# Sliding-window attention and a spectral mix on one core: whole-batch loads, 128x192 band tiles, weights stationary in the mode mix, and x@w_ch moved under the weight stream

## The chip, the core and the metric

The kernel runs on one core of one Trainium2 chip. The metric is device time in microseconds (us) from start to end of the program, and lower is better. The span that the profile shows is 1 to 3 us shorter than that time.

Engine names: PE is TensorE (matmuls), PEld its weight loads, DVE is VectorE, ACT is ScalarE, POOL is GpSimd, SP is SyncE. A matmul has a stationary operand, loaded into the array of 128 x 128 cells, and a moving operand whose columns are streamed through it. "Array shape 128x64" below means a stationary operand of 128 rows and 64 columns.

## What is computed

```python
# q, k, v: (8 batches, 8 heads, 576 positions, 64), fp32
scores = q @ k.T / 8;  keep only 0 <= i - j < 64;  attn = softmax(scores) @ v
x  = attn laid out as (8, 576, 512)
X  = rfft(x over positions)[:, :64]                   # 64 modes
Yr = Xr @ w_r[m] - Xi @ w_i[m];  Yi = Xr @ w_i[m] + Xi @ w_r[m]     # per mode m
y  = irfft(Y);  u = x + y
out = u + relu(u @ w_ch)                              # fp32, (8, 576, 512)
```

The weights w_r and w_i are 2 x 64 matrices of 512 x 512 in fp32: 128 tiles of 1 MiB, turned into bf16 by the loads. They are most of the traffic. No mode can be mixed before the last batch's DFT, because each mode needs all 8 batches.

## The kernel before

Three stages run one after the other. Line numbers such as L228 in the profile lines of before are those of this kernel.

```python
# ---- attention, per batch b and pair of heads hp (cut) ----
for hh in range(2):                       # q and k: rows of one token, 256 B each
    nc.gpsimd.dma_start(out=raw[:, :, hh, :],
        in_=src5[b, 2*hp+hh, 0:512, :].rearrange("(c t) d -> t c d", t=128))
for c in range(4):                        # L192: 128x128 transposes
    nc.tensor.transpose(out=ptr[:, c*128:(c+1)*128], in_=raw2, identity=ident_bf)
...                                       # v: fp32 by SP, then a cast on ACT
for c in range(5):                        # key blocks of 128, 256 queries each
    nc.tensor.matmul(out=pss[:nk, :nq], lhsT=kT[pp, q0:q0+nk], rhs=qT[pp, q0:q0+nq])   # L228
    nc.scalar.activation(out=et, in_=pss, func=Exp, scale=1/8)                         # L235
    nc.vector.tensor_tensor(out=et, in0=et, in1=m01, op=mult)                          # L237
for qb in range(5):                       # weigh v: two matmuls add into pso
    nc.tensor.matmul(out=pso, lhsT=et_c[:nk, 0:nq2], rhs=vt[:nk, qb, :], start=True, ...)      # L247
    nc.tensor.matmul(out=pso, lhsT=et_p[:nk, 128:128+nq2], rhs=vt[:, qb-1, :], stop=True)      # L253
    ...                                   # reciprocal, scale: one pair of DVE instructions each
# DFT: trigF stationary, x moving (512 columns), L267, then 4 transposes

# ---- mode mix: X stationary (16 columns), weights moving (512 columns) ----
for m in range(64):                       # 20 buffers for weight tiles
    nc.gpsimd.dma_start(out=wr, in_=moe_w_r[m]...)
    nc.gpsimd.dma_start(out=wi, in_=moe_w_i[m]...)
    for dch in range(4):
        nc.tensor.matmul(out=psm, lhsT=XQ[:, dch, m, B:3*B], rhs=wr[:, dch, :])   # L323
        nc.tensor.matmul(out=psm, lhsT=XQ[:, dch, m, 0:2*B], rhs=wi[:, dch, :])   # L325
    ...                                   # copy to SBUF, two 8 KB DMAs into Yall

# ---- tail, per batch and 128 positions ----
#  inverse DFT (L344), u = x + y on DVE (L350), 4 transposes of u (L353), copy on ACT,
#  4 products with w_ch (L360), out = max(., 0) + u on DVE (L367), store
```

The softmax here doesn't subtract the row's maximum and nothing guards it: scores larger than these inputs give would overflow.

## Time and profile before

| | before |
|---|---|
| time, median of 3 | 644.14 us (643.96 to 644.51) |
| last DFT product ends | 277.9 us |
| mode mix, first to last matmul | 280.0 to 562.5 us |
| tail (to the end of the span) | 562.5 to 641.3 us |
| matmuls | 2160 |

First the slices of the page: the span is cut into 40 equal slices of 16 us, and each digit is the busy share in tenths. PEclk is the clock that the throttle granted to TensorE, DMA the mean busy share of the 16 DMA engines.

```profile
PE   1798859787888888889555565665565555579997
PEclk9999999999999999999767888657888778889999
DMA  9999999999893942019999999999999999614333
```

One sees three stages, and a hole in the DMA row just before the middle one: all 20 weight buffers are full, and the stream can't go on before the last DFT.

Next, three stretches of before. The columns are the stretch in us, its length, then for each engine its busy time and the number of instructions, the granted clock (1.00 is full speed), the DMA share and the GB/s moved.

```profile
core 0: us, PE busy (x) PEld busy (x) DVE busy (x) ACT busy (x) POOL busy (x), PEclk, DMA share, GB/s
90.00:120.00 30.00, 26.01 (x154) 13.26 (x154) 18.86 (x113) 21.78 (x67) 20.02 (x38) 1.00 1.10 124
300.00:400.00 100.00, 58.14 (x180) 17.74 (x178) 0.00 (x0) 12.83 (x23) 21.13 (x40) 0.81 1.07 215
600.00:620.00 20.00, 19.94 (x105) 13.53 (x105) 16.28 (x26) 5.28 (x9) 0.00 (x0) 1.00 0.37 136
```

Attention keeps PE, ACT and DVE all fairly busy; the middle is full on DMA (share above 1 because packets overlap); the tail is full on PE.

The chain of waits (the work that ended last, followed back from the end) in the middle. The columns are start, length, and what the chain waited on; "issue" is a stretch in which the engine waited for nothing that the profile shows.

```profile
243.42 40.75 issue
...
287.67 9.89 DMA wi<-in_moe_w_i_dram
298.09 19.70 DMA wi<-in_moe_w_i_dram
318.32 19.59 DMA wi<-in_moe_w_i_dram
```

The chain is 40 us of nothing (the hole), then loads alone, 20.2 us for each 8 tiles here and 20.1 on average.

Last, single PE instructions of before in order of time: start, duration, line, what it writes and reads, array shape, moving shape, count. What matters is the distance between two starts, because matmuls are pipelined and the durations overlap.

```profile
121.52 0.24 PE L247 MATMUL pso<-vt,et 128*128 128x65 bf16 x1 [0.27 <-DVE x_sb L259]
121.57 0.25 PE L253 MATMUL pso<-vt,et 128*128 128x65 bf16 x1
...
122.99 0.26 PE L247 MATMUL pso<-vt,et 64*64 64x65 bf16 x1
123.18 0.26 PE L253 MATMUL pso<-vt,et 128*64 128x65 bf16 x1
123.37 1.03 PE L267 MATMUL psX<-x_sb,trigF 128*128 128x512 bf16 x2
```

Two matmuls of the same array shape start 0.05 us apart (121.52, 121.57). When the shape changes, the next one starts 0.19 us later (122.99, 123.18, 123.37), with the same 65 columns to stream.

### The profile page before, as it was taken

Reading aid. Unit: us, or ns where it says so; the run is one execution under the profiler, and the core shown is the slowest. Engines: PE = TensorE matmul, PEld = TensorE weight load, DVE = VectorE, ACT = ScalarE, POOL = GpSimd, SP = SyncE. Lnnn points to the kernel's source line nnn. Section 1 sums busy time; section 2 is a strip of 40 time slices with the busy share of each in tenths; the row PEclk is TensorE's granted clock in tenths of the full one; section 3 lists DMA queues with packets and bytes.
Section 4 is the critical chain, followed back from the end, with each engine's and each line's share of the span. In section 5 each row is a group of like instructions: output and inputs, shape, how many; then the busy total and the mean of one; then the engine's idle time right before and its main releaser. Section 6 shows DMA issues by size and latency. Waiting matters only on the chain.

```text
span 641.3 us, 7834 instructions
## 1 busy us (share of the span) xinstructions
PE 462.1 (72%) x2160; PEld 208.5 (33%) x2160; DVE 240.1 (37%) x1147; ACT 251.5 (39%) x671; POOL 214.6 (33%) x390
## 2 busy tenths in 40 slices
PE   1798859787888888889555565665565555579997
PEld 0344424433443434334111111111111111146664
DVE  4967736675677576820000000000000000048885
ACT  6976828594859597533111111111111111112222
POOL 9976564836581831013121221221211211000000
PEclk9999999999999999999767888657888778889999
DMA  9999999999893942019999999999999999614333
GB/s 144 108 136 141 200 140 119 139 208 173 88 108 35 106 45 28 2 33 216 215 214 214 215 214 215 214 215 214 214 214 214 215 214 214 138 50 143 137 133 131
DMA packets 142012, 98.05 MB, mean 153 GB/s; under 512 B 119440, under 2 KB 120464, under 8 KB 141968
## 3 DMA queue, kind: packets, MB, share of 16 engines
q0 software_dynamic: 95760, 77.62, 76.4%
q1 hardware_dynamic: 46208, 19.94, 12.6%
q8 instruction: 17, 0.28, 0.2%
q14 instruction: 27, 0.22, 0.1%
HBM read 163.58 MB, written 9.44 MB: 270 GB/s over the span
## 4 chain that ended last, share of the span: by engine, by line
DMA 48%; PE 28%; issue 10%; ACT 8%; DVE 3%; SPq 1%; POOL 1%; POOLq 0%; ACTq 0%
DMA wi<-in_moe_w_i_dram 41%; PE pss L228 6%; PE pout L360 6%; PE pstr L192 3%; DMA raw<-in_q_dram 3%; PE psut L353 3%; PE pso L247 3%; ACT et L235 3%; DMA raw<-in_k_dram 2%; DMA vs<-in_v_dram 2%; PE psy L344 2%; PE psX L267 2%; PE pso L253 2%; ACT qT L201 1%; ACT vt L215 1%
## 5 line engine op out<-in xcount | busy, mean ns | idle before, releaser
L325 PE MATMUL psm<-wi,XQ 128*16 128x512 bf16 x256 | 124.5, 486 | 93.5 <-DMA wi<-in_moe_w_i_dram 93.5
L323 PE MATMUL psm<-wr,XQ 128*16 128x512 bf16 x256 | 125.2, 489 | 18.1 <-DMA wr<-in_moe_w_r_dram 17.2
L350 DVE TENSOR_TENSOR ut<-x_sb,psy 128x512 f32<-128x512 bf16 (+1 forms) x40 | 27.1, 684 | 287.2 <-PE psy L344 285.8
L328 ACT CAST stg<-psm 16x512 bf16<-16x512 f32 x64 | 36.8, 575 | 243.7 <-PE psm L325 240.9
L235 ACT ACTIVATE et<-pss 128x256 bf16<-128x256 f32 (+2 forms) x320 | 94.0, 346 | 17.8 <-PE pss L228 9.1
L228 PE MATMUL pss<-qT 64*128 64x256 bf16 (+2 forms) x320 | 81.3, 344 | 11.9 <-ACT et L235 4.6
L323 PEld LDWEIGHTS <-XQ 128*16 128x16 bf16 x256 | 25.8, 101 | 186.1 <-issue 129.7
L247 PE MATMUL pso<-vt,et 128*128 128x65 bf16 (+1 forms) x320 | 72.8, 245 | 13.6 <-DVE x_sb L259 10.7
L319 POOL DMA_DIRECT2D wr<-in_moe_w_r_dram x64 | 34.5, 539 | 142.7 <-PE psm L323 66.3
L259 DVE TENSOR_SCALAR x_sb<-pso,rcp 128x64 bf16<-128x64 f32 (+1 forms) x320 | 76.7, 274 | 2.5 <-DVE rcp L258 1.6
L258 DVE RECIPROCAL rcp<-pso 128x1 f32<-128x1 f32 (+1 forms) x320 | 45.1, 156 | 72.1 <-PE pso L253 57.0
L237 DVE TENSOR_TENSOR et<-et,m_69 128x256 bf16<-128x256 bf16 (+2 forms) x320 | 69.1, 253 | 5.0 <-ACT et L235 4.3
L320 POOL DMA_DIRECT2D wi<-in_moe_w_i_dram x64 | 34.4, 537 | 97.9 <-DMA wi<-in_moe_w_i_dram 92.3
L192 PE MATMUL pstr<-ident_bf,raw 128*128 128x128 bf16 x256 | 43.2, 302 | 27.5 <-DMA raw<-in_k_dram 11.3
L253 PE MATMUL pso<-vt,et 128*128 128x65 bf16 (+1 forms) x256 | 61.1, 248 | 0.0
L247 PEld LDWEIGHTS <-et 128*128 128x128 bf16 (+1 forms) x320 | 36.0, 116 | 70.5 <-DVE x_sb L259 23.3
L186 POOL DMA_DIRECT2D raw<-in_q_dram x64 | 49.3, 781 | 22.1 <-PE pstr L200 16.7
L186 POOL DMA_DIRECT2D raw<-in_k_dram x64 | 49.4, 782 | 16.2 <-PE pstr L200 6.7
L360 PE MATMUL pout<-wch,utt 128*128 128x512 f32 (+1 forms) x160 | 43.6, 410 | 0.5 <-ACT utt L357 0.5
L325 PEld LDWEIGHTS <-XQ 128*16 128x16 bf16 x256 | 27.6, 108 | 44.4 <-issue 28.2
L215 ACT CAST vt<-vs 128x325 bf16<-128x325 f32 x61 | 28.2, 463 | 34.3 <-PE pso L253 27.5
L357 ACT CAST utt<-psut 128x512 fp32r<-128x512 f32 (+1 forms) x33 | 19.2, 581 | 53.9 <-PE psut L353 53.9
(82 smaller groups left out, 443.9 us busy)
## 6 DMA issues: line engine op xcount, KB each, us to landing
wr<-in_moe_w_r_dram POOLq DMA_DIRECT2D x64, 512.0 KB, 19.6
wi<-in_moe_w_i_dram POOLq DMA_DIRECT2D x64, 512.0 KB, 19.6
vs<-in_v_dram SPq DMA_DIRECT2D x64, 128.0 KB
out_dram<-ot SPq DMA_DIRECT2D x32, 256.0 KB
raw<-in_q_dram POOLq DMA_DIRECT2D x64, 64.0 KB, 3.2
raw<-in_k_dram POOLq DMA_DIRECT2D x64, 64.0 KB, 3.3
Yall<-stg SPq DMA_DIRECT2D x128, 8.0 KB
vs<-in_v_dram SPq DMA_DIRECT2D x64, 16.0 KB
```

Source lines behind the costliest of these rows:

```text
L186: nc.gpsimd.dma_start(out=raw[:, :, hh, :], in_=src5[b, 2 * hp + hh, 0:512, :].rearrange("(c t) d -> t c d", t=128),)
L192: nc.tensor.transpose(out=ptr[:, c * 128:(c + 1) * 128], in_=raw2, identity=ident_bf[:, :])
L228: nc.tensor.matmul(out=pss[:nk, :nq], lhsT=kT[pp, q0:q0 + nk], rhs=qT[pp, q0:q0 + nq], start=True, stop=True)
L235: nc.scalar.activation(out=et[:nk, :nq], in_=psss[hl][:nk, :nq], func=ACT_F.Exp, scale=EX_SCALE)
L237: nc.vector.tensor_tensor(out=et[:nk, :nq], in0=et[:nk, :nq], in1=m01[:nk, :nq], op=ALU.mult)
L247: nc.tensor.matmul(out=pso[:nq2, :], lhsT=et_c[:nk_c, 0:nq2], rhs=vt[:nk_c, qb, :], start=True, stop=(qb == 0))
L253: nc.tensor.matmul(out=pso[:nq2, :], lhsT=et_p[:nk_p, 128:128 + nq2], rhs=vt[:nk_p, qb - 1, :], start=False, stop=True)
L258: nc.vector.reciprocal(out=rcp[:nq2, :], in_=pso[:nq2, D:D + 1])
L259: nc.vector.tensor_scalar(out=x_sb[:nq2, b, qb, h * 64:h * 64 + 64], in0=pso[:nq2, 0:D], scalar1=rcp[:nq2, :], scalar2=None, op0=ALU.mult)
L323: nc.tensor.matmul(out=psm[:, :], lhsT=XQ[:, dch, m, B:3 * B], rhs=wr[:, dch, :], start=(dch == 0), stop=False)
L325: nc.tensor.matmul(out=psm[:, :], lhsT=XQ[:, dch, m, 0:2 * B], rhs=wi[:, dch, :], start=False, stop=(dch == NDCH - 1))
L360: nc.tensor.matmul(out=pout[:nt, :], lhsT=utt[:, ech * nt:(ech + 1) * nt], rhs=wch[:, ech, :], start=(ech == 0), stop=(ech == NDCH - 1))
```

## The change

The intent: load q, k and v of a whole batch in long runs; compute only a band of 192 queries for each 128 keys; keep the mode's weights in the array, so that Y comes out transposed; compute x@w_ch while the weights stream in, since (x + y)@w_ch = x@w_ch + y@w_ch; and do the last addition on GpSimd. The core of the diff, cut where dots stand, with comments added for this document:

```diff
-                    in_=src5[b, 2 * hp + hh, 0:512, :].rearrange("(c t) d -> t c d", t=128),
+                out=r, in_=src[b].rearrange("(x g) (p c) d -> (g p) x (c d)", g=2, c=RUN))   # 9 tokens a run
+                in_=vf[hp].rearrange("(j r c) d -> r j (c d)", j=9, r=32))                   # v: 4 tokens a run
...
+        def vmain(hp):                    # v into place: selection by matmul, 32 rows, 512 columns
+                pp = slice(32 * hp, 32 * hp + 32)
+                for c in range(4):
+                    nc.tensor.matmul(out=ps, lhsT=pick[pp, hp, c, :], rhs=rv[pp, 0:8, c, :],
+                                     start=(c == 0), stop=(c == 3))
...
+            for t in range(NT):           # weigh v (one of two groups of heads shown)
+                    if t < 4:
+                        mm(t, 128 * t, full, 0, 128, 0, t, True, t == 0)        # 128x128
+                    else:
+                        mm(t, 512, lo, 0, 64, 0, 4, True, False)                # 64x64
+                    if t:
+                        mm(t, 128 * t - 128, full, 128, 64, 0, t - 1, False, True)   # 128x64
+        nc.vector.reciprocal(out=rcp, in_=view(pso, D, [[512, 2], [D + 1, NT]]))  # 10 at once
...
+    EARLY = LW + EW                       # 8 + 10 weight tiles loaded during attention
...
-                nc.tensor.matmul(out=psm[:, :], lhsT=XQ[:, dch, m, B:3 * B],
-                                 rhs=wr[:, dch, :], start=(dch == 0), stop=False)
+                    nc.tensor.matmul(out=psy[:, m % MG, e, :], lhsT=wr[:, c, ee],
+                                     rhs=XQ[:, c, m, :, 1:3], start=(c == 0), stop=False)
...
+            if 10 <= m < 50:
+                channel(m - 10)           # 128 rows of x: 4 transposes, 4 products with w_ch, kept in Z0
...
-                    nc.tensor.transpose(out=psut[:, ech * nt:(ech + 1) * nt], ...
-                nc.vector.scalar_tensor_tensor(out=ot[:nt, :], in0=pout[:nt, :], scalar=0.0,
-                                               in1=ut[:nt, :], op0=ALU.max, op1=ALU.add)
+                nc.tensor.matmul(out=psc[:n, :], lhsT=trigI[:, ts], rhs=Yw, start=True, stop=False)
+                nc.tensor.matmul(out=psc[:n, :], lhsT=ident_r[:n, :n], rhs=Z0[:n, b, t, :], ...
+                nc.vector.tensor_tensor(out=u[:n, :], in0=psu[:n, :], in1=x_sb[:n, b, t, :], op=ALU.add)
+                nc.scalar.activation(out=r[:n, :], in_=psc[:n, :], func=ACT_F.Relu)
+                nc.gpsimd.tensor_tensor(out=ot[:n, :], in0=u[:n, :], in1=r[:n, :], op=ALU.add)
```

## The prediction

> **What bounds the kernel now.** The profile's stretches show three stages. (1) Attention and DFT, 0 to 283 us: per 30 us PE is busy 25 to 26, ACT 22, DVE 20. (2) Weight stream, 283 to 563 us: the chain of waits is all wi loads, 20.1 us per 8 tiles, 2.51 us per 1 MiB tile; 20 tiles were prefetched, 108 are left. DMA idles from 240 to 280 us (slices at 0 to 2 tenths): all 20 buffers are full and no mode can start before the last DFT. (3) Inverse DFT, transposes, x@w_ch, output, 563 to 641 us: PE busy 19.9 of 20.
>
> **What limits attention.** From starts of successive matmuls in the trace: same array shape 128x128, 65 columns: 0.048 us; 128-column transposes 0.06 to 0.1; but when the shape of the array tile changes (128x128 to 64x64, 64x128, 128x64) 0.17 to 0.19, more after wider matmuls. Before has 543 such changes in its 1287 attention matmuls.
>
> **What the change does.**
> - Attention: exp columns fall from 8,190 to 6,660 per batch. ACT and DVE need about 13 us per batch each. q/k/v come in runs nine times (v four times) longer: an estimated 70 us in all, off the path. But PE gets 1888 matmuls instead of 1287, and the order of instructions shows 604 shape changes, 475 of them inside the weighing of v (128x128 and 128x64 tiles alternate). I estimate 205 to 220 us of PE time, against 155 to 195 by the same count before. So attention becomes PE-bound at 26 to 30 us a batch and ends near 240 us (range 195 to 270) instead of 283: gained from fewer stalls, not from less PE work.
> - Stream: 18 tiles early, 110 left. The first reload waits for mode 5, so DMA starts about 10 us after the DFT. Mode mix with weights stationary: 32 matmuls of 16 columns at about 0.05 us = 1.6 us (twice that when throttled), plus x@w_ch at about 2 us, against 5 us of DMA per mode: stays DMA-bound. The 8 KB Y stores go away (4 of 256 us of queue time), so about 2.48 us per tile: 272 us.
> - Tail: per batch PE 4 transposes x 0.11 + 4 x 0.23 + 15 x 0.23 = 4.8 us, DVE 4.0 us, ACT 3.4 us. The final add moves to GpSimd. The Trainium skill, "GPSIMD Engine Reference", Performance versus the Vector engine, gives 4497 ns for a two-input fp32 add of 2048 columns; I estimate 1.1 us for 512, 40 of them 45 us. Tail about 50 us instead of 78, bound by GpSimd.
>
> **Sum.** 240 + 12 + 272 + 3 + 50 + 3 (time over span) = 580 us; shaded to 576. In 8 of 10: 528 to 616. Faster by over 2% 0.93, within 2% 0.05, slower 0.02.
>
> **Shown right or wrong by.** End of attention: 195 to 270 us with PE busy over 85% and gaps near 0.18 us in the weighing; the chain in the middle on weight DMA at 2.45 to 2.51 us per tile, PE clock above 0.75; a DMA hole before mode 5; GpSimd adds at 1.1 us, back to back, in the tail.
>
> **What would make it wrong.** If a change from 128x128 to 128x64 costs nothing, attention ends near 180 us and the total is about 515. If matmuls of 16 columns cost over 0.1 us or the clock stays halved while x@w_ch runs, the stream turns PE-bound and adds 20 to 60 us.

## The result, and the profile after

The changed kernel takes 605.80 us (median of 4, 602.99 to 606.65), against 644.05 us for the kernel before on the same chip. The ratio of the two is 0.942, with a 95% interval of 0.939 to 0.945. Ratios are the mean time of one kernel's fast runs over that of the other's of the same rounds, so they are not quite the ratio of the medians that are quoted.

| | before | after | difference |
|---|---|---|---|
| mode mix starts | 280.0 | 261.5 | -18.5 |
| mode mix, first to last matmul | 282.5 | 282.5 | 0.0 |
| from the last mode's matmul to the end | 78.8 | 60.8 | -18.0 |
| span | 641.3 | 604.9 | -36.4 |

The middle stage, where two of the five ideas were put to work, has kept its length to the tenth of a us. All the gain is in the first and the last stage. The slices, as for before:

```profile
PE   2998999999999999877878873222222222229883
PEclk9965555555555555559998995555555555558998
DMA  9999585848430000139999999999999999972554
```

Now PE is the engine at 90% all through attention, and the DMA row has a hole of five slices instead of three. The stretches of after, with the same columns:

```profile
core 0: us, PE busy (x) PEld busy (x) DVE busy (x) ACT busy (x) POOL busy (x), PEclk, DMA share, GB/s
110.00:140.00 30.00, 28.49 (x229) 16.79 (x228) 14.13 (x19) 13.08 (x16) 4.57 (x8) 0.50 0.64 106
200.00:230.00 30.00, 29.51 (x232) 17.62 (x231) 14.65 (x21) 12.63 (x16) 0.00 (x0) 0.50 0.00 1
320.00:360.00 40.00, 32.41 (x413) 22.56 (x412) 10.29 (x18) 9.34 (x16) 8.45 (x16) 0.91 1.06 213
400.00:440.00 40.00, 9.97 (x272) 8.52 (x273) 0.69 (x1) 0.00 (x0) 8.44 (x16) 0.50 1.06 213
560.00:580.00 20.00, 17.23 (x74) 11.61 (x75) 12.56 (x20) 9.90 (x19) 20.00 (x18) 1.00 0.54 192
```

ACT and DVE have fallen from about 22 and 19 us to 13 and 14 in 30; loads are done by 200 us; PE is at 28 to 29.5. In the stream DMA moves 213 GB/s with x@w_ch running (320 to 360 us) and without it (400 to 440 us). In the tail POOL is busy for 20.00 of 20 us.

The chain of waits around the start of the stream:

```profile
170.11 82.96 issue
253.09 0.80 POOL wch L365
253.89 13.08 issue
266.98 0.51 POOL wt L115
...
268.05 9.85 DMA wt<-in_moe_w_r_dram
...
281.43 16.30 DMA wt<-in_moe_w_r_dram
...
301.24 16.19 DMA wt<-in_moe_w_r_dram
```

From 281.43 to 301.24 is 19.8 us for 8 tiles, so 2.48 us a tile. The first reload goes out at 267 us, 5.5 us after the mix began, because its buffer is free only after the sixth mode.

PE's instructions in attention after:

```profile
115.38 3.11 PE L284 MATMUL pso<-vt_147,et 128*128 128x65 bf16 x18
...
120.38 2.99 PE L284 MATMUL pso<-vt_147,et 64*128 64x65 bf16 x18
...
126.39 1.88 PE L236 MATMUL psv<-rv,pick 32*128 32x512 bf16 x4
```

A group of 18 weighing matmuls takes 3.0 us and more, 0.17 us each, although a 65-column matmul needs 0.05. Four selection matmuls of v take 1.8 us.

To compare whole stages I added up, from the trace, the time from each PE instruction's start to the next one's start, without the time in which PE stood idle, up to the last DFT product:

| PE's time in attention (us) | before | after |
|---|---|---|
| weighing v (576 matmuls in both) | 77.9 | 94.6 |
| scores (320 in both) | 70.5 | 29.2 |
| transposes of q and k | 44.1 | 33.7 |
| putting v in place (128 of 512 columns, 128 of 64) | none | 51.7 |
| DFT, with what is transposed for it | 26.4 | 24.8 |
| PE idle between instructions | 51.0 | 13.5 |

PE has slightly more to do than before (234 instead of 219 us) and waits 37 us less. The last DFT product of after ends at 257.5 us: 8.3 us before PE's first instruction, 13.5 idle, these 234, and 1.6 for the first transposes of x@w_ch.

The scores fell most, by 41 us. They stream at most 192 columns instead of 256, and the matmuls of two heads, which use different halves of the array's rows, now stand side by side: many start in pairs less than 0.01 us apart (two at 123.30 us and two at 123.38 in the trace of after). This saving paid for more than half of the work that was added; no run tests it by itself.

### The profile page after: what moved, and what is told of

It is laid out like the page before. It is cut to its first block, busy times and chain, and to the rows that moved or that the text cites. A ratio compares the mean times of both kernels' runs of the same rounds, so it can differ in the third digit from the quotient of the medians.

```text
span 604.9 us, 10161 instructions
## 1 busy us (share of the span) xinstructions
PE 408.4 (68%) x4440; PEld 267.7 (44%) x4440; DVE 198.3 (33%) x317; ACT 166.4 (28%) x226; POOL 155.3 (26%) x230
## 4 chain that ended last, share of the span: by engine, by line
DMA 38%; issue 26%; PE 25%; POOL 5%; DVE 4%; ACT 1%; POOLq 0%; DVEq 0%; ACTq 0%
DMA wt<-in_moe_w_r_dram 33%; PE pso L284 9%; PE psv L236 5%; POOL ot L476 5%; DMA wt<-in_moe_w_i_dram 3%; PE pst L210 3%; PE pss L264 3%; PE psx L319 2%; DVE u L472 1%; DMA rq<-in_q_dram 1%; PE psw L245 1%; DVE Yb L459 1%; PE psu L466 1%; DVE x_sb L308 0%; DVE XQ L322 0%
## 5 line engine op out<-in xcount | busy, mean ns | idle before, releaser
L403 PE MATMUL psy<-XQ,wt 128*128 128x16 bf16 x1024 | 57.1, 174 | 94.8 <-DMA wt<-in_moe_w_i_dram 94.6
L400 PE MATMUL psy<-XQ,wt 128*128 128x16 bf16 x1024 | 59.6, 174 | 61.9 <-DMA wt<-in_moe_w_r_dram 58.4
L403 PEld LDWEIGHTS <-wt 128*128 128x128 bf16 x1024 | 46.1, 102 | 101.6 <-DMA wt<-in_moe_w_i_dram 101.4
L115 POOL DMA_DIRECT2D wt<-in_moe_w_r_dram x64 | 34.2, 535 | 218.5 <-PE psy L403 205.8
L284 PEld LDWEIGHTS <-et 128*64 128x64 bf16 (+3 forms) x576 | 61.2, 118 | 45.2 <-issue 9.8
L400 PEld LDWEIGHTS <-wt 128*128 128x128 bf16 x1024 | 46.4, 103 | 74.6 <-DMA wt<-in_moe_w_r_dram 69.4
L268 ACT ACTIVATE et<-pss 128x768 bf16<-128x768 f32 (+1 forms) x64 | 55.8, 903 | 23.8 <-PE pss L264 23.7
L476 POOL TENSOR_TENSOR ot<-u,r 128x512 f32<-128x512 f32 (+1 forms) x40 | 49.7, 1278 | 25.4 <-ACT r L474 25.4
L386 PE MATMUL psz<-wch,xT 128*128 128x512 f32 (+1 forms) x160 | 53.2, 456 | 1.8 <-DVE xT L383 1.4
L284 PE MATMUL pso<-vt_147,et 128*64 128x65 bf16 (+3 forms) x288 | 49.1, 251 | 1.8 <-DVE x_sb L308 0.9
L284 PE MATMUL pso<-vt_146,et 128*64 128x65 bf16 (+3 forms) x288 | 48.5, 249 | 0.4 <-DVE x_sb L308 0.4
L236 PE MATMUL psv<-rv,pick 32*128 32x512 bf16 x128 | 45.4, 598 | 2.5 <-ACT vt_146 L64 1.4
L115 POOL DMA_DIRECT2D wt<-in_moe_w_i_dram x64 | 35.1, 549 | 6.5 <-DMA wt<-in_moe_w_i_dram 3.7
```

What stands on the lines that cost most here:

```text
L115: nc.gpsimd.dma_start(out=wt, in_=src[m].rearrange("(p c) e -> p c e", c=NC))
L236: nc.tensor.matmul(out=ps, lhsT=pick[pp, hp, c, :], rhs=rv[pp, 0:8, c, :], start=(c == 0), stop=(c == 3))
L268: nc.scalar.activation(out=et, in_=ps[:, :, 0:w], func=ACT_F.Exp, scale=EX_SCALE)
L284: nc.tensor.matmul(out=pso[po:po + nq, hh, t * (D + 1):(t + 1) * (D + 1)], lhsT=et[pk, hh, col + c0:col + c0 + nq], rhs=vt[pk, hp, j, :], ...
L386: nc.tensor.matmul(out=psz[:n, :], lhsT=xT[:, c, 0:n], rhs=wch[:, c, :], start=(c == 0), stop=(c == NC - 1))
L400: nc.tensor.matmul(out=psy[:, m % MG, e, :], lhsT=wr[:, c, ee], rhs=XQ[:, c, m, :, 1:3], start=(c == 0), stop=False)
```

## The experiments

Each starts from the changed kernel (605.80 us) unless said otherwise. The runs of the kernel before beside them have medians of 642.6 to 643.3 us, so chips and rounds differ by no more than 0.3%. Twelve kernels were run.

### e1_order: the same weighing matmuls, ordered by array shape

The removed loop is summed up in one line, and only one of the two groups of heads is shown:

```diff
-            for t in range(NT):  ...  128x128 of t, then 128x64 of t, head by head
+            for mm in mms:                      # both heads: all 128x128
+                for t in range(4):
+                    mm(t, 128 * t, full, 0, 128, 0, t, t == 0, t == 0)
+            for mm in mms:                      # the 64x64 of both
+                mm(4, 512, lo, 0, 64, 0, 4, False, False)
+            for mm in mms:                      # all 128x64
+                for t in range(1, NT):
+                    mm(t, 128 * t - 128, full, 128, 64, 0, t - 1, False, True)
```

PSUM is the memory that matmuls write to; here each head has one of its banks. Only the first matmul in a head's bank now carries the start flag. A build that set it for every block, as the changed kernel does, gave infinities in the simulator and was not run. The Trainium skill, "PSUM — Partial Sum Buffer", The four PSUM rules, says that a matmul which starts a group clears the written marks of the whole bank, in the groups of 32 partitions that it writes, so that a group still open there is overwritten instead of added to. No run here shows that; with one flag the output was correct.

> The same 576 weighing matmuls, but all 128x128 tiles of a head pair first, then the 64-row ones, then all 128x64 tiles, so that about 3 instead of about 16 of 18 follow a tile of another shape. Theory A (a change of array shape costs about 0.11 us on top of the matmul, and PE is the limit of attention): 32 groups x 12 x 0.11 = about 42 us less; the 18 matmuls of a group take about 1.5 us instead of 2.9; the last DFT ends near 220 us instead of 258; total 560 to 575. Rival B (0.165 us is simply what a 65-column matmul with its own weight load takes at the halved clock, in any order): the groups keep 2.8 to 3.0 us and the total stays within 3 us of 606. Rival C (the groups get shorter, but PE then waits for DVE, ACT or loads): groups at 1.5 us, total over 590.

Measured: 554.57 us, ratio 0.862 (0.858 to 0.866). The last DFT product ends at 205.8 instead of 257.5 us. PE's weighing time falls from 94.6 to 41.2 us, with 62 instead of 470 neighbouring pairs of different shape. A group of 18 now reads so in the trace of this run, and the next instruction starts 1.25 us after it, where it took 3.04 in the changed kernel:

```profile
162.65 1.32 PE L284 MATMUL pso<-vt,et 128*128 128x65 bf16 x18
```

This is theory A. The 53.4 us that the weighing lost over 408 fewer changes is 0.13 us for each change. Theory B (the matmul simply takes 0.165 us) has fallen, and so has C: PE's idle time rose only from 13.5 to 23.0 us. The gain is some us above what I had expected; part of that is a clock that is no longer halved all the time in this run (0.50 to 0.67 in stretches of 30 us), since the selection matmuls, which were not touched, fell from 51.7 to 46.5 us too. The edit also moved the two additions into one block of PSUM apart and set fewer start flags. These rivals were not run by themselves, but the trace of before speaks against them: there, two matmuls of one shape that add into the same block, the first with the start flag, start 0.05 us apart (121.52 and 121.57 above).

### e2_vdirect and e6_vdirect3: v straight into place, without selection matmuls

```diff
-                out=rv[32 * hp:32 * hp + 32, :, :, :].rearrange("r j c d -> r j (c d)"),
-                in_=vf[hp].rearrange("(j r c) d -> r j (c d)", j=9, r=32))
+                out=vts[b % 3][:, hp, :, 0:D],          # of e6; e2 has b % 2, which is wrong
+                in_=vf[hp].rearrange("(j p) d -> p j d", p=128))
-        units += [vmain(hp) for hp in range(4)] + [vlast]
```

> v goes straight to its place by DMA in rows of one token (256 B read, 128 B written) instead of long runs followed by 256 selection matmuls. Theory A (PE is the limit of attention): 128 x 0.43 + 128 x 0.06 = about 62 us of PE work leave, last DFT ends near 195 us, total 540 to 555, although the loads of v cost twice the queue time (36,864 packets of 32 ns over 16 engines = 73 us instead of 36). Rival B (loads would become the limit; long runs were what freed attention): DMA share near 1 up to the end of attention, gain below 20 us, total over 585.

Measured for e2: 580.38 us, but the output was wrong (relative error 0.59), by a mistake of mine: with two places for v, batch b+2 was written into the place of batch b before the last group of b had been weighed. The run settles nothing by itself. The mended run has three places:

> The run with v loaded straight into place again, now with three places for v instead of two: in the first try the load of batch b+2 overwrote v of batch b before its last group was weighed, so its output was wrong. Expected: correct, and by theory A (PE-bound) the 44.1 us of 512-column and 7.6 us of 64-column selection matmuls leave PE's attention, but the first try already showed 35 us of PE idle instead of 13.5, so 20 to 35 us less than 606: total 570 to 585. Rival B (short rows of v are what made attention slow before): total over 590.

Measured for e6: correct, 565.46 us, ratio 0.880 (0.878 to 0.881). The last DFT product ends at 213.2 us, 44 us earlier, although v now comes in short rows, 128 B each in SBUF. The selection matmuls had taken 51.7 us of PE; most of the difference is PE's idle time, 19.8 instead of 13.5 us. This is theory A, with one thing that it left out: the copies of v out of PSUM, 23 us of ACT and DVE together, went as well. The long runs of v had gained nothing, since loads were not the limit of the changed kernel's attention, and had brought 256 matmuls. The gain is 5 us above the upper end of what I expected of e6, because the first try, which I had leant on, had waited for its two places (PE waits 7.6 us for loads of v in the trace of e2 and not at all in that of e6). Of the 44 us, 40 are left in the total: from the last addition to the end of the span e6 takes 8.5 us, and so do e10 and e12, where the changed kernel takes 5.0. Why is open.

This run also shows how the clock row misleads. The stretch from 120 to 150 us and one group of weighing from the trace of e6:

```profile
core 0: us, PE busy (x) PEld busy (x) DVE busy (x) ACT busy (x) POOL busy (x), PEclk, DMA share, GB/s
120.00:150.00 30.00, 28.86 (x263) 19.73 (x264) 16.81 (x22) 15.18 (x16) 6.18 (x8) 1.00 0.81 109
```

```profile
131.31 3.12 PE L258 MATMUL pso<-vt,et 128*128 128x65 bf16 x18
```

The clock reads 1.00, and yet the group takes just what it takes in the changed kernel, where the clock reads 0.50. The trace of e6 has its first clock record at 230 us; before the first record the profile shows full speed. The trace of before has its first at 286 us, that of after at 27 us. So a recorded mean clock need not tell the speed: the runs of before beside these experiments have recorded means from 0.76 to 0.92, at times within 0.5% of each other.

### e5_vfull: the selection matmuls over 128 rows instead of 32

```diff
-                    nc.tensor.matmul(out=ps, lhsT=pick[pp, hp, c, :], rhs=rv[pp, 0:8, c, :],
+                    nc.tensor.matmul(out=ps, lhsT=pick[:, hp, c, :], rhs=rv[:, 0:8, c, :],
```

> The 128 selection matmuls that put v in place run over all 128 rows of the array instead of a strip of 32 (the selection matrix is zero in the other rows, so the sums are the same): same count, same 512 columns, more of the array active and one array shape fewer. Theory A (a 512-column matmul takes 0.427 us at the halved clock and 0.216 us at full clock however many rows it uses, and the clock stays halved): no change, 0.43 us each, total within 6 us of 606, a few us less from fewer shape changes (26 of 604, about 3 us). Rival D (the clock is halved because so few rows of the array are active): recorded clock in attention rises clearly above 0.5, selection matmuls near 0.22 us, attention 20 us or more shorter.

Measured: 583.50 us, ratio 0.908 (0.906 to 0.909); correct. The last DFT product ends at 235.0 us, 22.5 us earlier, with the same number of matmuls, the same columns and more multiplications. The stretches of this run:

```profile
60.00:90.00 30.00, 29.49 (x259) 18.58 (x259) 15.81 (x23) 14.25 (x17) 5.58 (x9) 0.70 0.79 129
90.00:120.00 30.00, 28.79 (x253) 18.03 (x252) 16.68 (x24) 15.53 (x19) 5.59 (x9) 0.60 0.72 118
```

There are clock records all through these stretches, and they alternate between 0.50 and 1.00, where the changed kernel has 0.50 without a break from 33 to 272 us. Rival D has won over my theory. The selection matmuls fell from 51.7 to 41.0 us, the weighing, which was not touched, from 94.6 to 86.3, and the scores from 29.2 to 26.5: the whole array ran faster. That the selection over 128 rows raises the clock is shown by this one edit. Whether it is the number of rows or the array shape, which changed with it, is not shown, and neither is how the throttle counts; in e1 the clock rose a little with the rows unchanged.

### e3_addsplit, e7_pipe, e8_pipesplit: what bounds the tail

```diff
# e3 and e8: 12 of 40 additions as one DVE instruction
+                if t == 1 or (t == 3 and b % 2):
+                    nc.vector.scalar_tensor_tensor(out=ot[:n, :], in0=psc[:n, :], scalar=0.0,
+                                                   in1=u[:n, :], op0=ALU.max, op1=ALU.add)
# e7 and e8: transposes, y@w_ch and copies of batch b+1 issued after the third tile of batch b
+                if t == 2 and b + 1 < B:
+                    head(b + 1)
```

> 12 of the 40 final additions move from GpSimd (relu on ACT, add on GpSimd, 1.28 us) to one DVE instruction from PSUM (about 0.69 us). Theory A (GpSimd bounds the tail): GpSimd 28 x 1.25 = 35 us, DVE 28 + 8 + 5 = 41 us, PE 38: tail about 48 us instead of 60, total about 594. Rival B (the tail is bound by PE, by output stores or by latency per batch): tail stays at 57 to 60, total within 3 us of 606.

> Tail only: the transposes and products of the next batch are issued three tiles early, so that PE no longer waits for ACT's copy at each batch. Theory A (the tail runs at GpSimd's pace, 6.2 us a batch for 5 adds of 1.28 us, and PE's chain of 6.0 us is only second): within 3 us of 606. Rival B (PE's chain per batch is the limit): tail 60 to about 53 us.

> Tail only: the early issue and the 12 additions on DVE together. If the two limits lie right behind each other (GpSimd 6.2 us a batch, PE's chain 6.0 us), each alone gives 0 to 3 us and both together bring the batch to about 5.2 us (PE 5.0, DVE 5.2, GpSimd 4.4): tail about 50 us, total about 596. Rival: output stores (9.4 MB) or something else bound the tail, total stays over 601.

The tail is counted here from its first PE instruction, 0.8 us after the last mode's matmul; the last column is the time from the first to the last GpSimd add, over 8 batches.

| | time | ratio (95%) | tail | first to last GpSimd add, per batch |
|---|---|---|---|---|
| after | 605.80 | 0.942 (0.939 to 0.945) | 60.1 | 6.2 |
| e3_addsplit | 602.70 | 0.937 (0.934 to 0.940) | 57.8 | 5.9 |
| e7_pipe | 606.70 | 0.943 (0.939 to 0.947) | 59.8 | 6.2 |
| e8_pipesplit | 597.94 | 0.931 (0.929 to 0.934) | 53.2 | 5.4 |

Freeing GpSimd alone gives 2 us of tail, where theory A of e3 expected 12. Freeing PE's chain alone gives nothing. Both together give 7. So GpSimd is the limit of the changed kernel's tail, as its 20.00 of 20 us say, but PE's chain stood right behind it: in e3, PE waits for ACT's copy of y@w_ch once between two batches (seven times, 4.2 us in all, in the list of waits). The same stretch of the changed kernel, then of e8:

```profile
550.00:590.00 40.00, 35.04 (x152) 23.16 (x151) 24.41 (x37) 21.43 (x40) 39.87 (x33) 1.00 0.52 182
```

```profile
550.00:590.00 40.00, 35.09 (x153) 23.91 (x152) 32.46 (x52) 18.35 (x31) 32.32 (x26) 1.00 0.62 218
```

In e8 no engine is full any more. The expected total of 596 was met within 2 us, with some luck: the tail shrank by 7 us and not by 10, and attention, which was not touched, ended 3 us earlier in the profiled run.

### e4_early14: fewer weight tiles loaded during attention

```diff
-    EW = 10
+    EW = 6
```

> 4 fewer weight tiles prefetched (14 instead of 18). Theory A (DMA stands idle for about 85 us before the stream for want of buffers and the stream is bound by loads at 2.475 us per tile): 4 x 2.475 = +10 us, total about 616, minus about 1.6 us because the first reload can start two modes earlier. Rival B (the stream is bound by something else, or the prefetch only shifts waits): within 3 us of 606.

Measured: 614.86 us, ratio 0.958 (0.955 to 0.962), so 9.1 us more. Each tile that is not loaded during attention costs about one tile's load time. The stream is bound by loads, and the hole in the DMA row is time lost for want of buffers.

### e9_late: x@w_ch after the stream

```diff
-            if 10 <= m < 50:
-                channel(m - 10)
+        for i in range(B * NT):             # after the loop over modes
+            channel(i)
```

> x@w_ch (40 pieces of 4 transposes and 4 products of 512 columns) is computed after the last mode instead of during the stream. If it is hidden under the loads in the changed kernel, the stream keeps 2.475 us per tile (it needs 2.475 with and without it in the trace) and the whole piece is added at the end: PE 40 x about 1.5 us = 60 us or more, total 660 to 680. If it slowed the stream, the stream gets shorter and the total rises by clearly less than 60 us.

Measured: 605.63 us, ratio 0.942. This run says nothing about the question. Where the call stands in the source does not decide when the work runs: the scheduler gave PE exactly the same order of instructions as in the changed kernel, and the products with w_ch ran from 268 to 364 us again.

### e10_all, e11_allfull, e12_all12: the parts together

e10 is e6 with the ordered weighing of e1 and the tail of e8. e11 is e5 with the same two. e12 is e10 with 20 early tiles.

> Everything that helped, with v loaded straight into place: weighing ordered by shape, early issue and 12 additions on DVE in the tail. If PE is still the limit of attention: 257 - 52 - 44 = 162 us. The loads of attention by themselves need about 172 us of queue time (135 measured, v 73 instead of 36), so I expect loads to take over and the last DFT to end at 180 to 190 us, total 520 to 535.

> The same with the long runs of v kept and the selection matmuls over all 128 rows. Loads need 135 us, PE about 235 - 53 - 8 = 175 us and less where the clock rises: last DFT at 185 to 195 us, total 525 to 538. If this one is faster than the one with v straight into place, the long runs are worth their matmuls once PE is relieved; if slower, they are not.

> The run with v straight into place and two more early weight tiles (20 instead of 18; the space is freed by the selection matrix and the raw v). DMA idles before the stream in every run so far, so 2 x 2.475 = 5 us less than the same run with 18. If loads are already the limit of attention there is no idle time left to fill and the two are within 2 us.

| | time | ratio to before (95%) | last DFT product | PE idle in attention |
|---|---|---|---|---|
| after | 605.80 | 0.942 (0.939 to 0.945) | 257.5 | 13.5 |
| e11_allfull | 526.72 | 0.819 (0.816 to 0.822) | 185.9 | 28.5 |
| e10_all | 511.03 | 0.795 (0.792 to 0.798) | 166.2 | 30.4 |
| e12_all12 | 508.60 | 0.792 (0.788 to 0.796) | 168.4 | 30.5 |

All three were correct. e10 beats what I expected, because one argument was wrong: I had taken the 172 us of queue time of its loads for time on the clock. Packets of one engine overlap, and in e10 178 us of them fit into 130 us. So PE was still the limit, and 257 - 52 - 44 = 162 us was near the 166 measured. e11 came as expected; with PE relieved, the long runs of v are still not worth their selection matmuls. Between e12 and e10 the medians differ by 2.4 us and the intervals overlap, so neither the 5 us nor the nothing that I had offered is shown. e10 and e12 are the fastest versions found.

## Why the prediction was right or wrong

**The total** was forecast at 576 us in a range of 528 to 616, and 605.8 was measured: right, but 30 us high of the middle. Its own sum before rounding down was 580. Where the 26 us to that sum lie:

| term | predicted | measured |
|---|---|---|
| attention (last DFT product) | 240 | 257.5 |
| DFT to the end of the stream, with the wait for the first reload | 12 + 272 | 286.5 |
| tail, with its start | 3 + 50 | 60.8 |
| time over span | 3 | 1.8 |

**Attention becomes PE-bound, with fewer stalls but not less work: right.** PE has 234 us of work after and 219 before, and idles 13.5 instead of 51.0 us. e1 shows it from the other side: taking 61 us of PE's time away, 53 of them in the weighing, moves the end of attention by 52 us, while the work of ACT, DVE and loads stays as it is. e6 moves it by 44 us, with more queue time for the loads of v but without the copies of v.

**Shape changes cost 0.17 to 0.19 us: right, and shown by e1.** The weighing, with 475 changes (470 as neighbours in the trace), was the largest single cost of the new attention, 94.6 us, and 53 us of it were removed by little more than another order. The Trainium skill, "TensorEngine Tiling (Array Packing)", Key Properties, says: "Changing tiling mode (not just tile) drains the TensorE". The trace agrees that a change costs time, and gives the price. The prediction counted the changes as a cost, but did not see that they could be ordered away.

**The mis-sized term is PE's time in attention: 205 to 220 us predicted, 234 measured.** In that sum I had put the 512-column selection matmuls at 0.22 us, the distance between 512-column matmuls in the tail of before, and the 128-column DFT matmuls at 0.07. They measured 0.34 (44.1 us over 128) and 0.155 (24.8 over 160). The main reason is the clock: more than half of the selection matmuls that follow each other start 0.39 to 0.43 us apart; the mean is lower because others overlap in different rows or ran at the full clock before 33 us. Two DFT matmuls of one shape start 0.10 us apart; the rest of the 0.155 is the change to 64 rows and back for the last block of positions, 0.22 to 0.25 us each. In the stream of before, 512-column matmuls start 0.42 us apart in one place and 0.21 in another (PE instructions of before, first around 540 us, then around 544 us):

```profile
539.65 0.63 PE L323 MATMUL psm<-wr,XQ 128*16 128x512 bf16 x1
540.07 0.63 PE L325 MATMUL psm<-wi,XQ 128*16 128x512 bf16 x1
```

```profile
544.51 0.38 PE L323 MATMUL psm<-wr,XQ 128*16 128x512 bf16 x1
544.73 0.38 PE L325 MATMUL psm<-wi,XQ 128*16 128x512 bf16 x1
```

The records give 0.50 for the first and 1.00 for the second. The Trainium skill, "TensorE: Matmul & The Clock Gate", Part 1, has the same two speeds, 426.7 and 215.7 ns. In attention the two DFT matmuls of before, in the fence at the head of this document (123.37, two of 0.62 us in 1.03), also start 0.41 us apart: attention ran at the halved clock in the kernel before too, under a row of nines. I read the row and not the distances. By my account the other distances came from the same stage and so were right; these two did not.

**The stream: right.** 2.48 us a tile was forecast and measured. e4 shows that loads bound it. The first reload went out 9.4 us after the last DFT product (267.0 and 257.5), as forecast (about 10), but partly by luck: PE waited 3.4 us of it before the first mode, which the forecast doesn't name, and the six modes took 5.5 us where it has 1.6 each, since a pair of weight load and 16-column matmul takes 0.027 us, not 0.05. In the stream of after, four matmuls a row:

```profile
434.18 0.25 PE L400 MATMUL psy<-XQ,wt 128*128 128x16 bf16 x4
434.28 0.25 PE L403 MATMUL psy<-XQ,wt 128*128 128x16 bf16 x4
```

A mode takes PE 0.9 us instead of the 3.4 us of eight 512-column matmuls 0.42 us apart, both at the halved clock. That is much less than predicted, and worth nothing by itself in a stage that waits for loads. What it bought is room for x@w_ch, at an unchanged pace of loads. The forecast that the clock would stay above 0.75 in the stream was wrong (0.50 from 365 to 549 us) and without effect.

**The hidden x@w_ch: not tested.** The stream's pace with and without it in the trace says that it costs nothing there; what it would have cost at the end is open, since e9 did not move it.

**The tail: the limit was right, its size was off.** A GpSimd add took 1.28 us instead of the 1.1 that I had scaled from the skill's figure, 49.7 us in all, back to back. With 6 us before the first add and 5 after the last, that is the 60.8 us. That PE's chain would stand 0.3 us a batch behind it (6.2 and, in e3, 5.9) was not seen: e3, e7 and e8 show it.

## What to carry to other kernels

Group matmuls by the shape of their stationary operand: a change of shape cost 0.12 to 0.13 us here at the halved clock, more than the 65-column matmul itself, and another order of the same work was worth 51 us. Read PE's clock off the distance between equal matmuls of known width, because the clock row shows full speed where there is no record. When an engine is the limit, look for the one right behind it before counting on a gain, and when a stage waits for loads, don't count what is saved on PE there.

## What the Trainium skill lacked or had wrong

- "TensorEngine Tiling (Array Packing)", Key Properties, says that changing the mode drains the engine, without a cost. For 65-column matmuls the distance was 0.17 to 0.20 us with a change and 0.05 without at the halved clock, and mostly 0.12 and 0.03 in e11, which ran mostly at a higher clock.
- "TensorE: Matmul & The Clock Gate", Part 1, ties the clock to how busy PE is and advises against idle gaps of about 3 us. Here PE was busy 97% of the time from 50 to 230 us, with no idle gap over 1.2 us, and the clock stayed at 0.50 from 33 to 272 us. Using 128 instead of 32 rows in the selection matmuls raised it to 0.60 to 0.72 in stretches of 30 us. The page doesn't say that rows or the array shape count.
- "GPSIMD Engine Reference", Performance versus the Vector engine, has one size, 4497 ns for 2048 columns. For 512 columns it took 1.28 us on 128 partitions and the same on 64, where a quarter of the figure would be 1.12.
- No page that I read says that the profile shows full clock before the first clock record. In e6 it showed 1.00 up to 230 us over matmuls with the pace of the halved clock.
